# Feature DFT of an FNet branch as seven block products inside the attention, on one Trainium2 core

## The chip, the cores and the metric

The kernel runs on one core of a Trainium2 chip. The metric is device time in microseconds, from launch to end, as the median of several runs. TensorE (PE in the profile) multiplies, ScalarE (ACT), VectorE (DVE) and GpSimd (POOL) work elementwise, and SyncE (SP) issues nearly all DMA transfers from one queue, in order.

## The reference

Two branches read the same x (2048 tokens, 640 features) and are mixed by a gate per token.

```python
# A: attention with 32 heads of 20 features
qkv = x @ wqkv                       # 640 -> 3 x 640
scores = q @ k.T * 20 ** -0.5
a = softmax(scores) @ v              # per head, all 2048 x 2048 pairs
a = a.reshape(2048, 640) @ wo
# B: Fourier mixing, the DFTs given as matrices
re = x @ dft_hid_re.T                # 2048 x 640, the "feature DFT"
im = x @ dft_hid_im.T
b = dft_seq_re @ re - dft_seq_im @ im  # the "sequence DFT"
g = sigmoid((x * gate_w).sum(-1))
out = g * a + (1 - g) * b
```

All data are float32. A product of two such operands is made of three matmuls in the format fp32r: each operand is split into a high and a low part, and high x high, high x low and low x high are added in PSUM.

## The kernel before, in words

**The front (0 to 250 us).** x is loaded and split into eight blocks `x00` to `x13` (part z, token quarter t), laid out as 5 slices of 128 features by 512 tokens. Then come query and key rows for the first heads, the values (`v_pair`), and from 105.9 us the remaining 32 query/key tiles: `qk_tile` calls `qk_pairs`, where each of 15 pairs of matmuls has 64 features in the upper and 64 in the lower half of the array, with the sums in two PSUM banks. ScalarE copies one bank, VectorE adds the other, GpSimd makes high and low part (`split`), and SP stores both to `qk_scr` in HBM. Pair tiles (name `p`) have five buffers, the one-off `raw` tiles three, the split `part` tiles three, the wide weight tiles `wb` two.

Among these tiles stand the first ten (`HEAD`) of 64 feature-DFT tiles: `hid_first` runs `hid_tile`, 15 pairs of 320 columns for 128 tokens and a quarter of the outputs (half `hf` of the features, real or imaginary part `ri`). The result goes to `a_scr` in HBM. `tick` puts one score step of the row maxima (two matmuls at line 177, two maxima at line 179) into each tile, so that 43 (`LEAD`) steps are done when the attention begins.

**The attention (250 to 1841 us)** has 32 units (a pair of heads, half of the queries), in all 256 cycles of four score steps. The order of a cycle is written out by hand:

```python
ORDER = "emFemFFFFemFeFFmeFFemFFFmmFFmeeB"
```

"e" is a score matmul (line 912) whose exponential ScalarE takes (918); "m" is a score matmul for the row maxima of a later unit (177), reduced by VectorE (179); "F" is a share of the fills; "B" is the burst: the sixteen value matmuls of line 565 and up to two of the `extras`, the read-outs and additions that a fill has left. All "e" and "m" take turns in five PSUM banks, the fills have two of their own (`yp`).

The fills are, one after the other: the other 54 feature tiles (one cycle each), 7 products of the sequence DFT (168 cycles), which already works on halved operands with seven instead of eight block products (`PRODUCTS`), and 30 tiles of the output projection, one cycle each, the last `SLOW` = 4 of them two. From cycle 246 on no maxima are left and the order is `LATE`. `at_step` puts a DMA or an operation at a later score step, and `begin` and `end` call them. In the last feature cycles the first operands of the sequence DFT are loaded and split by GpSimd (`load_a_early`, `make_a_early`, `load_c`).

**The end (1841 to 1869 us)**: the last heads' normalization and the rest of the output projection.

Of the kernel before, what the change touches and what calls it, by code (L numbers as in the profile page):

```python
# [18 lines left out]
P = 128  # L19
# [24 lines left out]
MARKS = (7,)  # L44
HEAD = 10

# [13 lines left out]


LONG = (0, 0, 0, 0, 0, 0, 0)
FULL = 1
SLOW = 4
PRE = range(FULL, NS)
# [9 lines left out]
@with_exitstack  # L75
def mix_kernel(ctx: ExitStack, tc: tile.TileContext, xa, wqk, wb, cdft, wo, out):
    nc = tc.nc
# [19 lines left out]
    l_scr = dram.tile([NU, 4, 512], F32, name="l_scr")  # L97
    o_scr = dram.tile([D, S], F32, name="o_scr")
    m_scr = dram.tile([NU, P, 2, 32], F32, name="m_scr")

# [182 lines left out]

    def load_wqk(c):
        raw = raw_tile()[:, : ND * P].rearrange("p (d c) -> p d c", d=ND)
        sp.dma_start(raw, wqk[c])

        def finish():
            w = part_tile().rearrange("p z c -> p (z c)")[:, : 2 * ND * P].rearrange("p (z d c) -> p z d c", z=2, d=ND)
            split(w[:, 0], w[:, 1], raw, act, dve)  # L290
            wt[c] = w

        return finish
# [16 lines left out]

    stores, halves, hid_done = [], [], 0

# [4 lines left out]
    def qk_tile(c, t):  # L317
        if hid_done:
            return qk_pairs(c, t)
# [19 lines left out]

    def tick(pairs):  # L340
        if pairs in MARKS:
            run_s(min(step + 1, LEAD))

    def qk_pairs(c, t):
        w = wt[c]
        ps = two_banks()
        for d in range(ND):
            for z, (wz, xz) in enumerate(((0, 0), (0, 1), (1, 0))):
                for h in range(2):
                    r = slice(64 * h, 64 * h + 64)  # L350
                    pe.matmul(ps[h], w[r, wz, d], xs[xz][t][r, d], start=d == 0 and z == 0, stop=d == ND - 1 and z == 2)  # L351
                tick(3 * d + z + 1)
        if not halves:
# [31 lines left out]

    def hid_tile(i, read_out):
        j, st = divmod(i, NS)
        hf, ri = divmod(j, 2)
        yp[:] = two_banks() if i < HEAD else [new_y(0), new_y(1)]
        w = wt["b", 2 + j]  # L390
        t, cs = st // 4, slice(st % 4 * P, (st % 4 + 1) * P)
        for d in range(ND):
            for z, (xz, wz) in enumerate(((0, 0), (0, 1), (1, 0))):
                for h in range(2):
                    r = slice(64 * h, 64 * h + 64)
                    pe.matmul(yp[h][:, :HE], xs[xz][t][r, d, cs], w[r, wz, d, :HE],  # L396
                              start=d == 0 and z == 0, stop=d == ND - 1 and z == 2)
                if (d, z) != (ND - 1, 2):
                    yield
        a = raw_tile()[:, :HE]  # L400
        y0, y1 = yp[0][:, :HE], yp[1][:, :HE]

        def read():
            act.activation(a, y0, AF.Copy, scale=-1.0 if ri else 1.0)
            dve.tensor_tensor(a, a, y1, op=ALU.subtract if ri else ALU.add)  # L405

        read_out(read, (a_scr[ri, hf, st], a))
        yield


    def hid_first(i):
        def read_out(read, args):
            read()
            stores.append(args)

        for pairs, _ in enumerate(hid_tile(i, read_out)):
            tick(pairs + 1)

# [39 lines left out]
    for s in range(0, NS, 2):  # L458
        v_pair(1, s)
        if s == 0:  # L460
            fin = load_wb(2)
        if s == 6:
            fin()
            fin = load_wqk(order[1])
        if s == 12:
            fin()
            fin = load_wb(3)
    free[0] = range(2, 5)
    for n, c in enumerate(order):
        for t in range(4):  # L470
            m = 4 * n + t
            if m % 3 == 0 and hid_done < HEAD:
                hid_first(hid_done)
                hid_done += 1
            qk_tile(c, t)
            if m == 8:
                load_v(0)
            if t == 1:
                if n + 1 < len(order):
                    fin()  # L480
                if n + 2 < len(order):
                    fin = load_wqk(order[n + 2])
    free[0] = range(5)
    run_s(LEAD)
    flush()

    def make_gate():
# [13 lines left out]
    def a_tile(n, s):  # L501
        g, k = (n, s // 4), s % 4
        if g not in blocks or k in blocks[g][1]:
            b = 4 * n + s // 4
            blocks[g] = block(b % 2, b // 2).rearrange("p (k z c) -> p k z c", k=4, z=2), set()
        blocks[g][1].add(k)
# [6 lines left out]
    def load_c(g):  # L513
# [9 lines left out]
        def finish():  # L523
            c = cparts[g] = part_tile()
            if len(raws) > 1:
                pool.tensor_tensor(raws[0], raws[0], raws[1], op=ALU.add if PRODUCTS[n][0][1][0] > 0 else ALU.subtract)  # L526
            split(c[:, 0], c[:, 1], raws[0], pool, pool)

# [274 lines left out]
    goals, fins = {}, []  # L803
    def read_later(read, args):
        extras.append((now[0], read))
        at_step(now[0] + 2, functools.partial(sp.dma_start, *args))

    HID = 4 * NS - HEAD
    fills = itertools.chain(*(hid_tile(HEAD + g, read_later) for g in range(HID)), itertools.chain.from_iterable(dft_step(g) for g in range(NS * UNITS)),
                            itertools.chain.from_iterable(out_tile(tt, hf) for tt in PRE for hf in range(2)))  # L810

# [59 lines left out]
    def end(i):  # L871
        if i % 4 == 2:
            c = i // 4
            if c + HEAD in (NS, 2 * NS):
                at_step(i + 2, load_wb(3 + (c + HEAD) // NS, pool, pool))
            if c in (HID - 18, HID - 17, HID - 16):
                k = c - HID + 18
                load_a_early(6 * k, min(6 * k + 6, NS))
            if HID - 12 <= c < HID - 8 or HID - 8 <= c < HID - 4:
                at_step(i + 2, make_a_early)  # L880
                at_step(i + 4, make_a_early)
            if c in (HID - 7, HID - 5, HID - 3):
                at_step(i + 4, load_c((c - HID + 7) // 2))
        if i in LAST:
# [195 lines left out]
```

## Time and profile before

| | |
|---|---|
| median of 3 runs | 1871.31 us (1870.73 to 1871.7) |
| the profiled execution | 1871.24 us, span 1869.4 us, granted clock 0.999 |
| PE busy | 1859.3 us (99%), 18157 matmuls |
| DVE busy | 1468.8 us (79%) |
| ACT busy | 1223.4 us (65%) |
| POOL busy | 1077.1 us (58%) |
| DMA | 281.66 MB, mean 151 GB/s |

A row of groups gives line, engine, operation, output <- input, shapes and count, then busy time in us and mean ns of one, then the idle time of the engine before them and who ended it. A row of windows gives the stretch, its length, and for PE, PEld (weight loads), DVE, ACT and POOL the busy time and the count, then the granted clock, the DMA engines' mean busy share and GB/s; where it is taken for one line, only the engines of that line appear. A row of the timeline gives start and length in us of a merged run of instructions.

### The profile page before, as it was taken

What the parts mean: (1) busy time and instruction counts of PE and PEld (TensorE: products, weight loads), DVE (VectorE), ACT (ScalarE), POOL (GpSimd) and SP (SyncE); (2) the same over time, 40 slices, a digit from 0 to 9 for tenths busy, and PEclk for the clock granted to TensorE, in tenths of its full rate; (3) what the DMA queues carried; (4) which work ended last, traced back from release to release, by engine and by line L of the source; (5) the groups of instructions that cost most, each with busy time, mean ns of one, the idle gap of its engine ahead of it and who ended that gap; (6) DMA issues with size and microseconds to landing.
All of it is one profiled execution on the core that took longest, in us unless ns stands there. A gap on an engine that the chain in (4) does not pass through costs nothing. (4 is left out here: it accounts for less than half of the span.)

```text
span 1869.4 us, 46025 instructions
## 1 busy us (share of the span) xinstructions
PE 1859.3 (99%) x18157; PEld 1356.1 (73%) x18157; DVE 1468.8 (79%) x2436; ACT 1223.4 (65%) x2359; POOL 1077.1 (58%) x942
## 2 busy tenths in 40 slices
PE   9999999999999999999999999999999999999998
PEld 8988877777777677776777767777677776766665
DVE  4145679898988888888888888888888888889943
ACT  4221257777777677676776767767677676777785
POOL 1234421010046896566799899777789988634434
PEclk9999999999999999999999999999999999999999
DMA  7744341312325473536666576647476746342214
GB/s 234 181 136 149 140 135 45 88 53 75 108 73 194 146 239 113 164 124 190 207 185 220 174 255 184 175 132 198 147 237 197 209 163 203 114 101 78 63 44 152
DMA packets 182283, 281.66 MB, mean 151 GB/s; under 512 B 52799, under 2 KB 114367, under 8 KB 182067
## 3 DMA queue, kind: packets, MB, share of 16 engines
q1 hardware_dynamic: 181107, 276.75, 49.2%
q0 software_dynamic: 960, 1.97, 0.6%
q8 instruction: 143, 2.34, 0.5%
q14 instruction: 73, 0.60, 0.1%
HBM read 213.90 MB, written 64.57 MB: 149 GB/s over the span
## 5 line engine op out<-in xcount | busy, mean ns | idle before, releaser
L179 DVE TENSOR_REDUCE mx<-ps 128x1 f32<-128x512 f32 x2048 | 1297.9, 684 | 200.0 <-PE ps L177 179.7
L918 ACT ACTIVATE p<-ps 128x512 f32<-128x512 f32 x2048 | 1087.0, 599 | 423.8 <-PE ps L177 217.0
L177 PE MATMUL ps<-kst,qst 60*128 60x512 f32 x2048 | 782.7, 413 | 0.9 <-DVE mx L179 0.6
L912 PE MATMUL ps<-qst,kst 62*128 62x512 f32 x2048 | 699.1, 415 | 0.2
L646 PE MATMUL yp<-x,part 64*128 64x320 f32 x5376 | 642.7, 306 | 0.0
L646 PEld LDWEIGHTS yp<-x,part 64*128 64x128 f32 x5376 | 580.5, 186 | 7.5
L912 PEld LDWEIGHTS ps<-qst,kst 62*128 62x128 f32 x2048 | 333.4, 184 | 225.5 <-DVE mx L179 169.8
L565 PE MATMUL av<-p,v 128*21 128x512 f32 x4096 | 492.5, 596 | 0.0
L177 PEld LDWEIGHTS ps<-kst,qst 60*128 60x128 f32 x2048 | 372.7, 184 | 11.0 <-DVE mx L179 1.4
L117 POOL TENSOR_TENSOR part<-raw,part 128x1024 fp32r<-128x1024 f32 (+1 forms) x129 | 290.6, 2253 | 10.3
L565 PEld LDWEIGHTS av<-p,v 128*21 128x21 f32 x4096 | 95.6, 100 | 206.9 <-issue 205.9
L396 PE MATMUL yp<-wb,x 64*128 64x320 f32 x1920 | 228.5, 307 | 0.0
L526 POOL TENSOR_TENSOR raw<-raw,raw 128x1024 f32<-128x1024 f32 x77 | 185.9, 2414 | 43.7 <-DMA raw<-in_cdft 42.1
L116 POOL CAST part<-raw 128x1024 fp32r<-128x1024 f32 (+1 forms) x129 | 127.1, 986 | 140.3 <-PE yp L646 119.3
L396 PEld LDWEIGHTS yp<-wb,x 64*128 64x128 f32 x1920 | 204.7, 186 | 3.7 <-DVE raw L405 0.2
L595 POOL TENSOR_TENSOR o<-o,rb 128x512 f32<-128x512 f32 x31 | 40.2, 1295 | 150.4 <-ACT p L918 52.7
L717 PE MATMUL yp<-x,part 64*128 64x320 f32 x720 | 90.3, 309 | 0.0
L117 POOL TENSOR_TENSOR x<-araw,x 128x320 fp32r<-128x320 f32 x96 | 83.9, 874 | 7.7
L351 PE MATMUL ps<-x,part 64*128 64x512 f32 x630 | 84.0, 390 | 0.0
L717 PEld LDWEIGHTS yp<-x,part 64*128 64x128 f32 x720 | 77.7, 186 | 2.9
L351 PEld LDWEIGHTS ps<-x,part 64*128 64x128 f32 x630 | 65.4, 185 | 11.3
L734 POOL TENSOR_TENSOR x<-x,m 128x320 f32<-128x320 f32 x30 | 26.2, 873 | 80.1 <-DVE m L729 63.9
(92 smaller groups left out, 1150.5 us busy)
## 6 DMA issues: line engine op xcount, KB each, us to landing
raw<-in_cdft SPq DMA_DIRECT2D x192, 512.0 KB
araw<-a_scr SPq DMA_DIRECT2D x176, 160.0 KB
qk_scr<-p SPq DMA_DIRECT2D x40, 512.0 KB
kst<-qk_scr SPq DMA_DIRECT2D x90, 160.0 KB
qst<-qk_scr SPq DMA_DIRECT2D x90, 160.0 KB
a_scr<-raw SPq DMA_DIRECT2D x64, 160.0 KB
yt<-y_scr SPq DMA_DIRECT2D x64, 160.0 KB
y_scr<-yt SPq DMA_DIRECT2D x64, 160.0 KB
```

Of the source, the lines that this page charges most:

```text
L116: e1.tensor_copy(dst1, src)
L117: e2.tensor_tensor(dst2, src, f32(dst1), op=ALU.subtract)
L177: pe.matmul(ps, q[b : b + KROWS, qt * P : (qt + 1) * P], k[b : b + KROWS, kc * 512 : (kc + 1) * 512], start=True, stop=True)
L179: return lambda: dve.tensor_reduce(mx[n][:, h, qt, kc : kc + 1], ps, axis=AX.X, op=ALU.max)
L351: pe.matmul(ps[h], w[r, wz, d], xs[xz][t][r, d], start=d == 0 and z == 0, stop=d == ND - 1 and z == 2)
L396: pe.matmul(yp[h][:, :HE], xs[xz][t][r, d, cs], w[r, wz, d, :HE], start=d == 0 and z == 0, stop=d == ND - 1 and z == 2)
L526: pool.tensor_tensor(raws[0], raws[0], raws[1], op=ALU.add if PRODUCTS[n][0][1][0] > 0 else ALU.subtract)
L565: pe.matmul(av[32 * j : 32 * j + DH + 1, :], v[:, kt, h * (DH + 1) : (h + 1) * (DH + 1)], pp[qc][:, h, :], start=kt == 0, stop=kt == NS - 1)
L646: pe.matmul(yp[h][:, :HE], c[r, cz, cs], a[r, az], start=s == 0 and z == 0, stop=s == NS - 1 and z == 2)
L717: pe.matmul(yp[h][:, :HE], o[r, oz, d], wos[d, hf][r, wz], start=d == 0 and z == 0, stop=d == ND - 2 and z == 2)
L912: pe.matmul(pt, k[b : b + KROWS + 2, kt * P : (kt + 1) * P], q[b : b + KROWS + 2, qc * 512 : (qc + 1) * 512], start=True, stop=True)
L918: act.activation(pts[n, kt, qc][:, h], pt, AF.Exp, scale=float(DH) ** -0.5)
```

## The change

The feature DFT is written as one product of a 2 x 2 block matrix x (token half by feature half) with a 2 x 2 block matrix of weights (feature half by real or imaginary part), and that as seven products of sums of blocks, each added to up to two results. A product has 8 units (half `hf` of the outputs, `k` of four token tiles), 56 in all. With only 320 features to sum over, a unit works on two token tiles at once, one in each half of the array, in 15 pairs of the same matmul shape as before. None is ahead of the attention; the fills begin with them, one cycle each.

- Weights (right operands): `load_set` loads one or two blocks of each of 14 sets, GpSimd adds them, ScalarE and GpSimd split them, and they go to `w_scr`; this runs beside the query/key tiles. `load_right` brings a set back, once into each half of the partitions, four cycles ahead.
- Left operands: `load_left` loads one or two blocks of x (a new input `xh`), GpSimd adds and splits slab by slab, into the blocks of x that are free by then, one product ahead; the first one at the end of the front.
- Results: two of the four stay in SBUF (`acc`), the other two are kept in `a_scr`, loaded again for the second addition. The read-out multiplies by the product's sign: ScalarE reads one bank, VectorE the other; GpSimd adds. Bursts of the feature stage may run three extras.
- The front: `SLOW` is 2; 14 query/key tiles have two score steps (`TWICE`), so that 43 are done as before; the high part of a query/key tile is made by ScalarE instead of GpSimd, the low part of the query/key weights by GpSimd instead of VectorE; the last eight tiles are taken in another order, the token quarters 2 and 3 first.
- The first operands of the sequence DFT are loaded and split later, in the last nine feature cycles, and lie in other blocks.

The core of the diff:

```diff
-HEAD = 10
+TWICE = range(2, 16)
+FEATURE = (
+    (((1, 1, 1),), ((1, 1, 0), (-1, 0, 0)), 1.0, ((1, 0, 0), (1, 1, 0))),
+    (((1, 0, 0), (1, 1, 1)), ((1, 0, 0), (-1, 1, 1)), 1.0, ((1, 0, 0), (1, 1, 1))),
+    (((1, 1, 0), (1, 1, 1)), ((1, 0, 0),), 1.0, ((1, 1, 0), (-1, 1, 1))),
+    (((1, 0, 0),), ((1, 1, 1), (-1, 0, 1)), 1.0, ((1, 0, 1), (1, 1, 1))),
+    (((1, 0, 0), (1, 0, 1)), ((1, 1, 1),), -1.0, ((-1, 0, 0), (1, 0, 1))),
+    (((1, 0, 1), (-1, 1, 1)), ((1, 1, 0), (-1, 1, 1)), 1.0, ((1, 0, 0),)),
+    (((1, 1, 0), (-1, 0, 0)), ((1, 0, 0), (-1, 0, 1)), 1.0, ((1, 1, 1),)),
+)
+SETS = 2 * len(FEATURE)
+RW = ND * HE
-SLOW = 4
+SLOW = 2
...
-        split(st[:, 0].bitcast(R), st[:, 1].bitcast(R), raw, pool, pool)
+        split(st[:, 0].bitcast(R), st[:, 1].bitcast(R), raw, act, pool)
...
+    def load_set(k):
+        _, terms, _, _ = FEATURE[k // 2]
+        w = wide.tile([P, 2, ND, BW], R, name="wb", bufs=2).rearrange("p z d c -> p (z d c)")
+        half = RW // 2
+        raws = [f32(w)[:, half * i : half * i + half] for i in range(2)]
+        for raw, (_, dh, ri) in zip(raws, terms):
+            sp.dma_start(raw, wr[ri, dh, k % 2])
+        def add():
+            if len(terms) > 1:
+                pool.tensor_tensor(raws[0], raws[0], raws[1], op=ALU.add if terms[1][0] > 0 else ALU.subtract)
+        def finish():
+            split(w[:, 2 * half : 3 * half], w[:, 3 * half : 4 * half], raws[0], act, pool)
+            stores.append((w_scr[k].rearrange("z r (q c) -> (r q) z c", q=2),
+                           f32(w)[:, 2 * half : 4 * half].rearrange("p (z c) -> p z c", z=2)))
+    def load_right(k):
...
+        for h in range(2):
+            sp.dma_start(f32(w)[64 * h : 64 * h + 64], w_scr[k].rearrange("z r c -> r z c"))
...
+    def hid_pair(u):
+        n, hf, k = u // 8, u // 4 % 2, u % 4
+        _, _, factor, targets = FEATURE[n]
+        ps = [new_y(z)[:, :HE] for z in range(2)]
...
+        for d in range(ND):
+            for a, b in ((0, 0), (0, 1), (1, 0)):
+                for z in range(2):
+                    r = slice(64 * z, 64 * z + 64)
+                    pe.matmul(ps[z], lefts[n][a][r, d, k * P : k * P + P], rights[2 * n + hf][r, b, d],
+                              start=done_ == 0, stop=done_ == 3 * ND - 1)
...
+        def read():
+            act.activation(m[:, 0], ps[0], AF.Copy, scale=factor)
+            dve.tensor_scalar(m[:, 1], ps[1], factor, 1.0, op0=ALU.mult, op1=ALU.mult)
+        def add(sign, old):
+            pool.tensor_tensor(old, old, m, op=ALU.add if sign > 0 else ALU.subtract)
+        extras.append((now[0], read))
+        last = n == len(FEATURE) - 1
+        for (sign, th, ri), new, row, old in zip(targets, fresh, rows, olds):
+            if not new:
+                extras.append((now[0] + 3, functools.partial(add, sign, old)))
+            if th != ri or ri == 0 and n == len(FEATURE) - 2 or ri == 1 and last:
+                at_step(now[0] + (4 if new else 8), functools.partial(sp.dma_start, row, m if new else old))
...
+    tiles = [(n, t) for n in range(6) for t in range(4)] + [(n, t) for t in (2, 3, 0, 1) for n in (6, 7)]
+    for m, (n, t) in enumerate(tiles):
+        qk_pairs(order[n], t, m)
+        if m == 8:
+            load_v(0)
+        if sets:
+            sets[0][m % 2]()
+            if m % 2:
+                sets.pop(0)
+            elif 2 <= m < 2 * SETS - 2:
+                flush()
+                sets.append(load_set(m // 2 + 1))
+        if n < 6 and t == 1:
+            fin()
+            if n + 3 < len(order):
+                fin = load_wqk(order[n + 3], pool)
+        if m == 27:
+            slabs = load_left(0, raw_stage)
+        if m in (28, 30):
+            flush()
+            load_right((m - 28) // 2)
+        if m >= 27:
+            slabs.pop(0)()
...
-    HID = 4 * NS - HEAD
+    HID = 8 * len(FEATURE)
...
+                if c % 4 == 0 and 2 <= c // 4 + 1 < SETS:
+                    at_step(i + 1, functools.partial(load_right, c // 4 + 1))
+                if k == 0 and n + 1 < len(FEATURE):
+                    slabs.extend(load_left(n + 1, own_stage))
+                if slabs:
+                    slabs.pop(0)()
...
-        run_extras(max(done - HIDS, 0) // 3, 2)
+        run_extras(max(done - HIDS, 0) // 3, 3 if c <= HID else 2)
```

More of the change, by code (lines that the diff above doesn't have):

```diff
@@ L526, in finish, with load_c_first @@
                 pool.tensor_tensor(raws[0], raws[0], raws[1], op=ALU.add if PRODUCTS[n][0][1][0] > 0 else ALU.subtract)
+            split(c[:, 0], c[:, 1], raws[0], pool, pool)
+        return finish
+    c_raws = []
+    def load_c_first(g):
+        if not c_raws:
+            w = f32(wide.tile([P, 2, ND, BW], R, name="wb", bufs=2)).rearrange("p z d c -> p (z d c)")
+            c_raws.extend(w[:, 1024 * q : 1024 * q + 1024] for q in (0, 1, 2, 0))
+        (_, th, ri), (sign, th2, ri2) = PRODUCTS[0][0]
+        raws = [c_raws.pop(0) for _ in range(2)]
+        for raw, (half, part) in zip(raws, ((th, ri), (th2, ri2))):
+            o = (2 * part + g % 2) * 1024
+            sp.dma_start(raw, cdft[half * HT + g // 2, :, o : o + 1024])
+        def finish():
+            c = cparts[g] = part_tile()
+            pool.tensor_tensor(raws[0], raws[0], raws[1], op=ALU.add if sign > 0 else ALU.subtract)
             split(c[:, 0], c[:, 1], raws[0], pool, pool)
```

171 lines of the change are left out of this document (100 added, 71 removed).

## The prediction

> **What bounds the kernel now.** I read the page first (slices, groups), then windows over the bursts of the value product (line 565: sixteen matmuls end each cycle of the attention), then one cycle in the timeline, then the front.
>
> ```profile
> span 1869.4 us, 46025 instructions
> PE   9999999999999999999999999999999999999998
> DVE  4145679898988888888888888888888888889943
> POOL 1234421010046896566799899777789988634434
> ```
>
> TensorE is busy everywhere, which doesn't say that it sets the pace everywhere. The windows of line 565, each beginning just ahead of a burst:
>
> ```profile
> 257.30:507.80 250.50, 76.89 (x640) 14.78 (x640) 1.00 0.28 79
> 526.52:589.20 62.68, 19.20 (x160) 3.73 (x160) 1.00 0.40 123
> 589.20:1650.30 1061.10, 322.91 (x2688) 62.13 (x2688) 1.00 0.60 179
> 1650.30:1785.00 134.70, 42.31 (x352) 8.11 (x352) 1.00 0.32 84
> 1796.00:1805.78 9.78, 3.89 (x32) 0.76 (x32) 1.00 0.25 67
> 1810.38:1836.96 26.58, 11.49 (x96) 2.79 (x96) 1.00 0.38 100
> ```
>
> Divide each stretch by its bursts (x640 is 40): feature cycles with 15 pairs of fill matmuls take 6.26 us, those at the end of that stage, beside a busy GpSimd, 6.27; sequence-DFT cycles with 16 pairs 6.32; output cycles with 12 pairs 6.12. Four pairs more or less move a cycle by 0.2 us, so the pairs are mostly filling. In the last cycles no maxima are left: 4.89 us with 12 pairs, 4.43 with 6. One feature cycle in the timeline:
>
> ```profile
> 269.79 1.92 PE L565 MATMUL av<-p,v 128*21 128x512 f32 x16
> 269.83 1.28 DVE L179 TENSOR_REDUCE mx<-ps 128x1 f32<-128x512 f32 x2
> 270.81 0.45 ACT L404 ACTIVATE raw<-yp 128x320 f32<-128x320 f32 x1
> 271.29 0.49 DVE L405 TENSOR_TENSOR raw<-raw,yp 128x320 f32<-128x320 f32 x1 [0.19 <-ACT raw L404]
> ...
> 271.64 0.51 PE L177 MATMUL ps<-kst,qst 60*128 60x512 f32 x1
> ...
> 272.20 5.13 DVE L179 TENSOR_REDUCE mx<-ps 128x1 f32<-128x512 f32 x8 [0.42 <-PE ps L177]
> ```
>
> Eight maxima run without a gap for 5.13 us (0.64 each); then VectorE has 1.09 us, from 271.11 to 272.20, in which it can get no new maximum because TensorE is in the burst. The read of the feature tile (0.49) lies in that hole. 5.13 + 1.09 is the cycle: VectorE's maxima and the burst set it.
>
> The front is different. From 105.9 to 250.0 us come 32 query/key tiles and ten feature tiles:
>
> ```profile
> 133.84 1.29 PE L396 MATMUL yp<-wb,x 64*128 64x320 f32 x13
> ...
> 147.34 1.29 PE L396 MATMUL yp<-wb,x 64*128 64x320 f32 x13
> ```
> ```profile
> 238.76 1.77 PE L351 MATMUL ps<-x,part 64*128 64x512 f32 x14
> 240.36 0.40 PE L177 MATMUL ps<-kst,qst 60*128 60x512 f32 x2
> 240.60 2.01 PE L351 MATMUL ps<-x,part 64*128 64x512 f32 x16
> 242.44 1.77 PE L351 MATMUL yp<-x,part 64*128 64x512 f32 x14
> ```
>
> Here TensorE runs without holes: a query/key tile with its one score step takes 242.44 - 238.76 = 3.68 us, the step in it 0.24, and one feature tile with three query/key tiles 147.34 - 133.84 = 13.50. What TensorE no longer does here is time saved.
>
> **The sum, part by part.** *Ten feature tiles leave the front.* One costs 13.50 - 3 x 3.68 = 2.46 us, less its score step, which only moves to another tile (43 steps before and after): 2.22. Ten: -22.2. The weight halves 2 and 3 are no longer split there, and with them goes one stall:
>
> ```profile
> 117.53 3.32 DVE L117 TENSOR_TENSOR wb<-raw,wb 128x966 fp32r<-128x966 f32 x2 [0.21 <-ACT wb L114]
> ...
> 121.50 0.18 PEld L177 LDWEIGHTS ps<-kst,qst 60*128 60x128 f32 x1 [0.94 <-DVE mx L179]
> ```
>
> VectorE split weights until 120.85, its maxima came late and TensorE waited 0.9: -0.9. The tile stretch shrinks from 144 to 121 us.
>
> *The feature stage.* Seven products of 8 units, 15 pairs each, are 840 pairs instead of 960; but the cycles count, not the pairs. It takes 56 cycles instead of 54, the end gives back two (only the last two output tiles, not four, get two cycles). Two output cycles become feature cycles: 2 x (6.26 - 6.12) = +0.3. Four late cycles get 12 pairs instead of 6: 4 x (4.89 - 4.43) = +1.8.
>
> *A unit's read-out.* Now ScalarE and VectorE each read one bank, neither waiting for the other; VectorE's operation changes from 0.49 to the kind of the second row:
>
> ```profile
> L405 DVE TENSOR_TENSOR raw<-raw,yp 128x320 f32<-128x320 f32 x64 | 31.1, 486 | 11.8 <-ACT raw L404 11.8
> L728 DVE TENSOR_SCALAR m<-yp,gate 128x320 f32<-128x320 f32 x7 | 3.9, 551 | 39.3 <-PE yp L717 36.2 <-PE ps L912 3.1
> L358 DVE TENSOR_TENSOR p<-p,ps 128x512 f32<-128x512 f32 x21 | 14.4, 687 | 23.7 <-ACT p L357 23.7
> L117 POOL TENSOR_TENSOR p<-p 128x512 fp32r<-128x512 f32 x32 | 42.2, 1320 | 2.6
> L117 POOL TENSOR_TENSOR part<-raw,part 128x512 fp32r<-128x512 f32 x15 | 19.4, 1290 | 1.2
> L116 POOL CAST part<-raw 128x512 fp32r<-128x512 f32 x15 | 9.2, 613 | 10.9 <-PE yp L646 5.7 <-PE ps L912 3.7 <-PE ps L177 1.4
> L117 POOL TENSOR_TENSOR part<-raw,part 128x640 fp32r<-128x640 f32 x1 | 1.6, 1568 | 0.1
> L117 POOL TENSOR_TENSOR wb<-raw,wb 128x966 fp32r<-128x966 f32 x2 | 4.5, 2275 | 0.2
> ```
>
> 0.55 in a hole of 1.09 costs nothing; without that cover it would be 56 x 0.06 = 3.4. Nor does the wait that goes (0.19) give anything, since the next maximum waits for TensorE. A rule speaks against this operation beside a GpSimd that is now busy. The Trainium skill ("SBUF — State Buffer", Who interferes with whom) says that a tensor-scalar operation of VectorE in its two-port mode and GpSimd shut each other out of the shared port; "VectorE: DVE Perf Modes" (Mode 2×_2P) restricts that mode to operands in SBUF, and this one reads a PSUM bank. The row fits the restriction: 551 ns for 320 columns is no faster than the two-input kind.
>
> *GpSimd in the feature stage.* A unit's add to an old result, 128x640, takes 1.57 us; a half-operand slab of 128x512 takes 1.29 for the sum of two blocks and 0.61 + 1.29 for the split. The fullest product with slabs (the fifth) has 16 adds, 5 slabs and one normalization: 25.1 + 16.0 + 1.3 = 42.4 us in its 8 x 6.26 = 50.1. Operands are ready two cycles ahead of their use, sums have a cycle before they are stored. So it is hidden; the two feature windows above (6.26 and 6.27) show that a busier GpSimd doesn't move the cycle. I take +1, with 0 and 5.6 (0.1 per cycle) as ends; fewer pairs show 0.14 less per cycle, so -3 as the end below. What queues behind a waiting SP instruction: the store of a sum waits for GpSimd, and the loads of the next heads and of the row of maxima stand behind it; but it is issued two cycles after the unit, a cycle after its add.
>
> *What the front gains in load.* Fourteen weight sets are loaded, added, split, stored to HBM. GpSimd: 32 low parts at 1.32, 24 operations of 128x800 at about 1.9 (an estimate between the 640 and 966 rows), six weight splits at 1.57, five slabs at 1.9: 42 + 46 + 9 + 10 = 107 of 121 us. VectorE in a tile with two steps: 4 x 0.64 + 0.69, plus some 0.6 in which its add waits for ScalarE's copy: 3.9 us beside TensorE's 3.68 + 0.24 = 3.92. Both fit barely. The DMA is tighter: 32 stores of 512 KB (16.8 MB), 20 block loads of 0.41 (8.2), 14 set stores of 0.82 (11.5), six weight tiles (2.0), values, first left operand and two duplicated right operands (4.9): 43.4 MB in 121 us, 359 GB/s.
>
> ```profile
> 105.90:249.60 143.70, 143.11 (x1353) 122.72 (x1354) 87.19 (x136) 28.71 (x51) 63.08 (x62) 1.00 0.39 141
> 23.00:33.00 10.00, 9.55 (x58) 8.83 (x58) 5.27 (x6) 5.28 (x9) 0.00 (x0) 1.00 0.96 359
> 904.00:924.00 20.00, 20.00 (x205) 14.32 (x202) 16.80 (x27) 14.14 (x27) 17.86 (x14) 1.00 0.86 295
> ```
> ```profile
> qk_scr<-p SPq DMA_DIRECT2D x31, 512.0 KB
> ```
>
> The front now moves 141 GB/s. The best ten microseconds of the trace reach 359, with 512 KB loads and stores like those here; a 20 us stretch of smaller packets 295. At 359 nothing is lost; at 295 the front takes 147 us, +26. On SP, which issues everything in order, each set load waits until the set two before it has landed in HBM, and the query/key stores queue behind that; they have five buffers of pair tiles, over two tiles (7 us) of grace. I take +2, near the 359 row because the transfers are of its kind; ends 0 and +26. "DMA: Bandwidth & Descriptors" in the Trainium skill (Specifications) gives 358 GB/s from HBM per core; by that figure the transfers would need 121 us, the same as TensorE, and the +2 would stand.
>
> *The joint.* The last slab of the first left operand comes after the last tile, some 5 us of GpSimd work (its low part, two slabs) before the twelfth pair of the first unit needs it: about even, +1 (0 to 3).
>
> Sum: -22.2 - 0.9 + 0.3 + 1.8 + 1 + 2 + 1 = -17.0. The profiled execution took 1871.24 us (1.8 outside its span), 0.07 below the median of 1871.31. Forecast 1854, in a range of its own from 1846 (no front loss, no joint, -3 in the feature stage) to 1859.
>
> **Rivals.** *The front becomes DMA-bound* (the one that ends slower): it decides below 43.4 MB / (121 + 19) us = 310 GB/s. At 295 the +2 becomes +26: 1878. For it: nothing in the trace holds 359 for more than about ten microseconds, and a load that waits for a store to land leaves a hole on the only queue. Against it: the buffers' grace and the sets with a single block. Half way, 310 to 345 GB/s, 1860 to 1867; around 310 nothing changes.
>
> *GpSimd sets the cycle in the feature stage*: if two adds and a slab (3.14 + 3.2 = 6.3) run in series with the unit's read (0.45), 6.8 instead of 6.26 in the 15 such cycles of three products, +8: 1862. For it, the sums; against it, three cycles without slabs in each product.
>
> *VectorE sets the front*: 0.35 us more in each of the 14 tiles with two steps: +5, 1859.
>
> *The port is locked after all*: each read waits for a GpSimd add or is waited for, 0.55 + 1.57 - 1.09 = 1.0 per cycle, 56 of them: 1910. The row at 551 ns speaks against it. The Trainium skill's rule of the shared port is its ground.
>
> **How the numbers follow.** A measurement of this kernel can tell about 0.2% (3.7 us) from no change. Forecast 0.64, front half bound 0.08, GpSimd 0.05, VectorE 0.04: faster 0.81. Front bound at about 310 GB/s: same 0.05. Front bound below that 0.10, port 0.04: slower 0.14. The range 1846 to 1868 takes in all the faster cases and leaves out 0.19.
>
> **What would show it.** Right: attention begins near 227 us, TensorE without waits in the front, windows of line 565's successor at 6.26 to 6.3 us a cycle in the feature stage. Wrong: TensorE or ScalarE in the front waiting behind pair tiles, a DMA share near 0.9 there with tiles over 3.9 us; feature cycles over 6.4 us; a wait of the score matmuls for left operands or for the row of maxima.

## The result, and the profile after

| | before | after |
|---|---|---|
| median | 1871.35 us (1870.73 to 1871.7) | 1895.83 us (1891.53 to 1901.53) |
| profiled execution, span | 1871.24, 1869.4 us | 1897.29, 1895.5 us |
| granted clock | 0.999 | 0.990 |
| DMA | 281.66 MB | 348.81 MB |

The ratio is 1.0133 (95% interval 1.0105 to 1.0161): slower by 24 us where 17 less were forecast. Four points of the trace divide the spans: the first score matmul (front before it, joint behind it), the first burst of the value product (line 701 in the new kernel), burst 56, and the last one. In us against the kernel before; the last column is a kernel that stands at the end of the experiments:

| stage | forecast | after | last kernel |
|---|---|---|---|
| front, to the first score matmul (before: 250.0) | -21.1 | -10.9 | -21.8 |
| joint, to the first burst (before: 7.3) | +1 | +9.1 | +5.8 |
| 56 feature cycles against the first 56 before (350.9) | +1.3 | +27.6 | +1.0 |
| cycles 56 to 246 | 0 | +1.5 | +1.7 |
| the rest | +1.8 | -1.2 | -0.9 |
| sum | -17.0 | +26.1 | -14.2 |

The front and the joint gave 18 us less than forecast, and the feature cycles lost 26. The windows of line 701 (columns: PE, PEld, granted clock, DMA share, GB/s) show that these cycles aren't slower as such:

```profile
297.00:391.10 94.10, 28.77 (x240) 5.61 (x240) 1.00 0.62 158
397.40:417.00 19.60, 5.23 (x32) 0.91 (x32) 0.83 0.75 220
497.30:531.90 34.60, 9.52 (x64) 1.58 (x64) 0.85 0.76 214
633.90:1696.00 1062.10, 322.90 (x2688) 61.98 (x2688) 1.00 0.62 181
```

Fifteen bursts in 94.10 us are 6.27 each, as forecast; the sequence DFT has its 6.32. But the next rows take 19.6 us for two cycles (22 and 23, counted from zero by the burst that begins them) and 34.6 for four. The first of them, engine by engine (PE, PEld, DVE, ACT, POOL):

```profile
397.40:403.40 6.00, 6.00 (x62) 4.18 (x60) 5.23 (x10) 4.57 (x9) 0.69 (x1) 1.00 0.80 194
403.40:409.40 6.00, 0.90 (x8) 0.43 (x7) 2.00 (x4) 0.04 (x1) 4.91 (x4) 0.67 0.49 137
409.40:413.20 3.80, 3.80 (x23) 1.04 (x24) 0.01 (x1) 1.80 (x4) 2.06 (x3) 0.62 0.82 263
```

TensorE does nearly nothing for 5 us, and then the clock is 0.62: 23 matmuls fill 3.80 us. (The Trainium skill, "TensorE: Matmul & The Clock Gate", Part 1, has the clock halved after an idle window of some 3.4 us; the rows agree, and so a wait costs more than its own length: the two cycles take 7.1 us more than plain ones, TensorE stood for 5.1 of it.) The waits (engine, line, releaser; total, times, longest) name what was late, and SP's queue says why:

```profile
PE ps L1052 <- DMA qst<-m_scr: 13.1, 3, 6.7
SPq L489 <- DMA a_scr<-part: 31.5, 8, 8.2
```
```profile
388.57 0.41 SPq L991 DMA_DIRECT2D a_scr<-part  x1
389.07 2.82 SPq L423 DMA_DIRECT2D wb<-w_scr  x2
393.22 0.37 SPq L489 DMA_DIRECT2D part<-a_scr  x1
393.68 0.93 SPq L991 DMA_DIRECT2D a_scr<-part  x1
394.70 0.42 SPq L724 DMA_DIRECT2D r_scr<-lc  x1
395.17 0.42 SPq L234 DMA_DIRECT2D m_scr<-m  x1
403.40 0.37 SPq L489 DMA_DIRECT2D part<-a_scr  x1
403.82 0.46 SPq L991 DMA_DIRECT2D a_scr<-part  x1
404.37 2.85 SPq L240 DMA_DIRECT2D qst<-m_scr  x4
```

Read it backwards. A unit's score matmuls need its row of maxima, which goes to HBM (`m_scr`) and comes back into `qst`. The matmul waits for this row (line 240), issued at 404.37 although its data were stored at 395.17. Ahead of it in SP's order stands the load of an old sum (489), which waits until 403.40 because the sum that lay in its place, stored at 393.68, has not landed. That store stands in the DMA behind the right operand, two transfers of 800 KB issued at 389.07. The DMA is full meanwhile, at a low rate:

```profile
392.00:399.00 7.00, 7.00 (x82) 4.61 (x74) 6.46 (x13) 5.17 (x11) 3.08 (x2) 1.00 1.01 222
```

The row is late three times. Cycles 22, 23, 38 and 39 carry 16.6 of the 27.6 us that the feature cycles take more than the kernel before's, the waits and the slow clock behind them. Cycle 35 carries 4.9: there VectorE stands 3.7 us for the row of the exponentials' sums (`lc`, line 721), which also comes through SP. Cycle 4 carries 3.5 for which the profile names no releaser.

In the front SP stands in the same way, at the set loads (line 404):

```profile
SPq L404 <- DMA w_scr<-wb: 47.4, 12, 6.1
ACT wb L128 <- POOL wb L408: 25.0, 6, 7.8
```
```profile
200.57 0.41 SPq L329 DMA_DIRECT2D w_scr<-wb  x1
201.07 0.84 SPq L329 DMA_DIRECT2D qk_scr<-p  x1
205.02 0.85 SPq L404 DMA_DIRECT2D wb<-in_wr  x2
205.97 0.38 SPq L329 DMA_DIRECT2D qk_scr<-p  x1
206.44 0.41 SPq L329 DMA_DIRECT2D w_scr<-wb  x1
206.95 1.00 SPq L329 DMA_DIRECT2D qk_scr<-p  x1
213.44 0.82 SPq L404 DMA_DIRECT2D wb<-in_wr  x2
```

A set goes out at 206.44; the next load into its tile is issued only at 213.44. GpSimd's add is then late, ScalarE stands for it (25.0 us in all) with the next query/key tile's copy behind, and TensorE runs out of PSUM banks, while the DMA isn't full (columns: all five engines, clock, DMA share, GB/s):

```profile
195.00:220.00 25.00, 18.36 (x139) 13.95 (x137) 7.94 (x13) 6.83 (x11) 14.44 (x10) 0.93 0.77 267
```

### The profile page after: what moved, and what is told of

The parts are those of the page before. It is cut to its first block, busy times and chain, and to the rows that moved or that the text cites. A ratio compares the mean times of both kernels' runs of the same rounds, so it can differ in the third digit from the quotient of the medians.

```text
span 1895.5 us, 45927 instructions
## 1 busy us (share of the span) xinstructions
PE 1853.7 (98%) x17917; PEld 1340.8 (71%) x17917; DVE 1453.8 (77%) x2420; ACT 1248.2 (66%) x2392; POOL 1293.3 (68%) x1092
## 2 busy tenths in 40 slices
DMA packets 205820, 348.81 MB, mean 184 GB/s; under 512 B 54319, under 2 KB 124079, under 8 KB 205603
## 5 line engine op out<-in xcount | busy, mean ns | idle before, releaser
L131 POOL TENSOR_TENSOR part<-raw,part 128x1024 fp32r<-128x1024 f32 (+3 forms) x134 | 296.9, 2216 | 15.0 <-ACT part L128 4.8
L496 PE MATMUL yp<-wb,x 64*128 64x320 f32 x1680 | 212.6, 312 | 7.7 <-POOL p L131 4.5
L130 POOL CAST part<-raw 128x1024 fp32r<-128x1024 f32 (+2 forms) x127 | 125.0, 984 | 134.1 <-PE yp L782 102.6
L496 PEld LDWEIGHTS yp<-wb,x 64*128 64x128 f32 x1680 | 183.7, 190 | 11.7 <-POOL p L131 4.8
L509 POOL TENSOR_TENSOR x<-x,raw 128x640 f32<-128x640 f32 x40 | 62.4, 1561 | 39.5 <-DVE raw L506 30.8
L363 PE MATMUL yp<-x,part 64*128 64x512 f32 x480 | 66.0, 398 | 7.2 <-ACT p L369 6.0
L676 POOL TENSOR_TENSOR araw<-araw 128x320 f32<-128x320 f32 x80 | 69.9, 874 | 1.9 <-DMA araw<-a_scr 1.9
```

The costliest lines, as they stand in the source:

```text
L130: e1.tensor_copy(dst1, src)
L131: e2.tensor_tensor(dst2, src, f32(dst1), op=ALU.subtract)
L496: pe.matmul(ps[z], lefts[n][a][r, d, k * P : k * P + P], rights[2 * n + hf][r, b, d], start=done_ == 0, stop=done_ == 3 * ND - 1)
```

## The experiments

The theory: SP's one queue is blocked in two ways, by a load that waits until a store out of the same place has landed, and by a slow block that stands in the DMA ahead of small transfers. The rivals: the bytes alone fill the DMA (V), or GpSimd is the late engine (G). Each time below is the median of 4 to 10 executions; but for a single outlier, those of one kernel lie up to 14 us apart, so that a difference of a few us between two medians says little. In the code, `...` stands for lines that are not shown.

**Fixed set tiles.** The two tiles are taken once and used by region, so that a block load waits only for the split that read its region.

```diff
...
-        w = wide.tile([P, 2, ND, BW], R, name="wb", bufs=2).rearrange("p z d c -> p (z d c)")
+        if k < 2:
+            set_tiles.append(wide.tile([P, 2, ND, BW], R, name="wb", bufs=2).rearrange("p z d c -> p (z d c)"))
+        w = set_tiles[k % 2]
```

> The right operand's sets use two tiles by region for the whole front: a set's blocks load into the first half of a tile as soon as the split of two sets before has read it, and no longer wait for that set's store to land. Theory T: the front's 12 us of stalls come from SP standing at the block load until the store has landed (34.8 us on SP in seven places), GpSimd's add being late and ScalarE's first part standing in front of the next tile's copy: 1882 to 1887, the first score matmul at 227 to 230 us instead of 239. Rival V (the front's bytes fill the DMA): 1891 to 1901, with the stalls on other waits. Rival G: GpSimd's add and split (4 us and more per set) are the limit, no change.

1886.02 us, ratio 1.0081 (1.0066 to 1.0096), 9.8 us less. The first score matmul comes at 228.4 instead of 239.1, and the same window has TensorE busy and the DMA at its full share:

```profile
195.00:220.00 25.00, 24.02 (x207) 21.24 (x205) 11.65 (x18) 9.59 (x16) 19.70 (x14) 1.00 1.03 382
```

The whole kernel moves the same 348.81 MB as the changed one: the order of the queue, not the bytes, held the front. All kernels below but the next have this edit. In the profiled executions of the nine kernels that have this edit and practically the same front, the first score matmul comes at 228.3 to 233.1 us, so that up to 5 us in a single trace's front say nothing about an edit.

**The row of maxima on GpSimd's queue** (on the changed kernel).

```diff
+        rq = sp if now[0] < 0 else pool
...
-            sp.dma_start(m_scr[n], f32(m))
+            rq.dma_start(m_scr[n], f32(m))
... # and rq for the row's four loads
```

> Within the attention the row of maxima (its store and its four loads) is issued by GpSimd's queue instead of SP's; nothing else changes. Theory T (SP's order, not the DMA, holds the row): the score matmuls' wait for the row (13.1 us in three places) and the slow bursts behind it go, some 20 us; what is left is the wait for the reciprocal's row (3.7 us) and the front; 1872 to 1880. Rival V (DMA too full): the row lands as late from another queue, 1891 to 1901. Rival G (GpSimd is the late engine): its queue gives the row even later, over 1897.

1945.96 us, ratio 1.0397 (1.0380 to 1.0415). The waits:

```profile
POOL qst L242 <- DMA m_scr<-m: 64.3, 22, 7.1
PE ps L1054 <- DMA qst<-m_scr: 43.0, 11, 10.0
```

GpSimd now stands for the landing of the row's own store, and the row is later still. The time lies where rival G put it (over 1897), but by a wait that the edit itself brought: the run doesn't decide between them.

**Later loads of old sums**: three steps after the pair's begin, stores two steps earlier.

```diff
-                sp.dma_start(old, row)
+                at_step(now[0] + 3, functools.partial(sp.dma_start, old, row))
...
-                at_step(now[0] + (4 if new else 8), ...
+                at_step(now[0] + (4 if new else 6), ...
```

> On top of the fixed set tiles (1886.0 us), the load of an old sum is issued three steps after its pair's begin and not at it, and a sum is stored two steps earlier, so that five steps (7.8 us) and not none lie between a store and the next load of the same place; bytes and engines are as they were. Theory T, part Q (SP stands at the load until the store before it has landed, 24.8 us in six waits, and the rows of maxima and of sums of the exponentials stand behind): the waits for the row of maxima (13.2 us) and the slow bursts behind them go, 1866 to 1872. Part D alone (the rings are held): the rows are late all the same, 1882 to 1889. Rival V: 1882 to 1889.

1894.56 us: 8.5 *more*. Of the 12.3 us between the two profiled executions 6.4 are in the feature cycles; 4.4 are in the front, which the edit doesn't touch. The waits for the row stay (14.2 us in three places). In cycle 22 SP stood instead at a sum's store, which waits for GpSimd's add, which waits for the old sum: its load was issued at 379.48, behind the right operand, and the add began at 389.86. Without the wait at line 489 the row is as late; the block in front is enough to hold it.

**Right operands in two transfers over all partitions**, the rows of one part read for both halves.

```diff
-        for h in range(2):
-            sp.dma_start(f32(w)[64 * h : 64 * h + 64], w_scr[k].rearrange("z r c -> r z c"))
+        for z in range(2):
+            sp.dma_start(f32(w)[:, z], w_scr[k, z : z + 1].to_broadcast([2, 64, RW]))
```

> On top of the fixed set tiles (1886.0 us), each right operand is fetched by two transfers over 128 partitions (the high parts, then the low parts; the source rows read twice), in place of two over 64 partitions of the same bytes. Theory T, part D (the transfers over half the partitions run at half rate and hold the rings for about 7.5 us): the stalls of the feature stage (cycles 22, 35, 38 and 54, some 21 us over the plain 6.25) shrink by half, 1873 to 1879. If only SP's order matters (part Q), no change: 1883 to 1889. Rival V (volume): no change.

2190.67 us, ratio 1.1706 (1.1685 to 1.1727): a failed experiment, for a reason of its own, so that it says nothing about the theory. A window within such a transfer:

```profile
381.00:400.00 19.00, 11.76 (x115) 7.81 (x112) 11.11 (x19) 9.22 (x18) 9.70 (x9) 0.93 0.13 53
```

A share of 0.13 is two engines of sixteen. (The Trainium skill, "DMA: Bandwidth & Descriptors", Why a DMA increments its semaphore by 16 and not by 1, says that a transfer uses the largest number of engines up to 16 that divides the slowest dimension of both sides; here the source's is 2, and the share agrees.) The two kernels that held the same transfer, with later loads and with an earlier joint, took 2195.56 and 2197.91 us and tell nothing more.

> Both edits on top of the fixed set tiles: later loads of old sums and right operands over 128 partitions. Theory T: 1864 to 1870, a little under the better of the two, since both shorten the same wait. Rival V: 1880 or more.

> As the kernel with both edits, and the first left operand's slabs and the first two right operands start one token tile earlier in the front, so that they are there when the first feature pair starts. Theory T: the 7 to 9 us that lie between the first score matmul and the first value matmul beyond the kernel before's 7.3 shrink by 3 to 6 us: 1859 to 1866. Rival: the front's DMA is full there (share over 1.0 from 195 us on) and the tiles before it lose what the joint gains: within 1.5 us of the kernel without it.

**The same bytes over 128 different rows**, which puts half of them where another part belongs, so that the kernel doesn't give the wanted output and only prices the transfer; and three ways to move the block in time or place:

```diff
# 128 rows, in wrong places
+        for j in range(2):
+            sp.dma_start(f32(w)[:, j], w_scr[k].rearrange("z r c -> (z r) c"))
# four pieces: half h, part z
+        for j, (h, z) in enumerate(itertools.product(range(2), range(2))):
+            args = f32(w)[64 * h : 64 * h + 64, z], w_scr[k, z]
...
+                at_step(now[0] + 3 * j, functools.partial(sp.dma_start, *args))
# GpSimd's queue (rq is GpSimd within the attention)
+            rq.dma_start(f32(w)[64 * h : 64 * h + 64], w_scr[k].rearrange("z r c -> r z c"))
# two cycles later
-                if c % 4 == 0 and 2 <= c // 4 + 1 < SETS:
+                if c % 4 == 2 and 2 <= c // 4 + 1 < SETS:
```

> On top of the fixed set tiles, each right operand is fetched by two transfers of 800 KB over 128 different rows and 128 partitions; the rows are put in the wrong places, so that the operand is not the one wanted; bytes, packets and queue are as before. Theory B with the half rate as its cause: the block takes 4.5 to 5 us and not 8 to 9, the waits for the row of maxima (13.2 us) halve or go, 1868 to 1878. If 64 or 128 partitions make no difference: 1882 to 1889.

> On top of the fixed set tiles (1886.0 us), each right operand is fetched in four pieces of 400 KB (half of the partitions, one part each), three steps (4.7 us) apart, in place of 1.6 MB at once; same bytes, still over 64 partitions. Theory B (a block of 1.6 MB at some 210 GB/s stands in the queue's rings for 8 to 9 us; the sums' stores and loads behind it land late, SP stands for them in order, and the row of maxima behind SP comes late): a piece holds the rings for 2 us, the four long cycles (22, 35, 38, 54; some 21 us) shrink to a few us, 1866 to 1873. Rival V (the DMA's volume, whatever its order): 1882 to 1889. Rival Q (SP's order and waits alone, however the blocks lie): 1880 to 1889.

> On top of the fixed set tiles, the right operands' loads within the attention are issued by GpSimd's queue instead of SP's, so that they stand in rings of their own. Theory B (the order within the queue's rings is what delays the small transfers): sums and rows go past the block, 1866 to 1874. If the sixteen engines are full for the block's time whichever queue it comes from: 1882 to 1889. Rival G: GpSimd stands for the tile to come free and its adds are late: 1885 or more.

> On top of the fixed set tiles, each right operand's load is issued two cycles later (two cycles before its first use and not four), behind the row of maxima of the units in question and not ahead of it. Theory B: cycles 22 and 38, which wait for the row (some 16 us with the slow bursts behind them), become plain ones; 1868 to 1877. Rival V: 1882 to 1889; a late operand (score pairs waiting for it) would show as TensorE waiting for the operand's load, over 1889.

The 128 rows: 1863.49 us, ratio 0.9962 (0.9946 to 0.9978), 22.5 us less than the fixed sets and faster than the kernel before, with the same bytes. In the profiled executions 18.6 us of the gain are in the feature cycles. The waits of the fixed sets (first two rows) and of this kernel:

```profile
PE ps L1056 <- DMA qst<-m_scr: 13.2, 3, 6.9
SPq L493 <- DMA a_scr<-part: 32.2, 8, 8.1
```
```profile
PE ps L1056 <- DMA qst<-m_scr: 1.6, 1, 1.6
SPq L493 <- DMA a_scr<-part: 26.1, 8, 4.1
```

The longest wait of SP for a sum's landing is halved, and the row is hardly late any more. The others (pieces, GpSimd's queue, later load) took 1892.41, 1896.99 and 1909.27 us, none less than the fixed sets' 1886.02. What TensorE waits for in them:

```profile
PE yp L504 <- DMA wb<-w_scr: 27.9, 7, 10.1
PEld yp L504 <- DMA wb<-w_scr: 23.8, 4, 10.5
```
```profile
PE yp L500 <- DMA wb<-w_scr: 40.8, 14, 5.8
```

The first two rows are the pieces, the third the later load. In both, cycles 22 and 38 are plain (6.26 to 6.27 us): the block did hold the row. But at its rate the operand then comes too late itself. On GpSimd's queue TensorE still waits for the row (16.2 us in three places) and GpSimd stands 29.3 us for the operand's tile to come free. So what helped was the rate, and none of these places. Volume (V) is out here, since the bytes are the same, and so is GpSimd (G), whose work is the same too.

**Why the rate.** Two other ways to fill both halves: the halves on two queues at once, or three parts in the scratch (high, low, high), of which rows 0 to 127 and 64 to 191 are fetched; the other half of the array then finds the parts exchanged.

```diff
# two queues
-            sp.dma_start(f32(w)[64 * h : 64 * h + 64], w_scr[k].rearrange("z r c -> r z c"))
+            q = sp if h == 0 or now[0] < 0 else act
+            q.dma_start(f32(w)[64 * h : 64 * h + 64], w_scr[k].rearrange("z r c -> r z c"))
# three parts
-    w_scr = dram.tile([SETS, 2, 64, RW], F32, name="w_scr")
+    w_scr = dram.tile([SETS, 3, 64, RW], F32, name="w_scr")
... # the high part is stored a second time
+        for j in range(2):
+            sp.dma_start(f32(w)[:, j], w_scr[k, j : j + 2].rearrange("z r c -> (z r) c"))
...
-                    pe.matmul(ps[z], lefts[n][a][r, d, k * P : k * P + P], rights[2 * n + hf][r, b, d],
+                    pe.matmul(ps[z], lefts[n][a][r, d, k * P : k * P + P], rights[2 * n + hf][r, b ^ z, d],
```

> On top of the fixed set tiles (1886.0 us), the upper half of each right operand within the attention is issued by ScalarE's queue and the lower half by SP's, so that the two transfers over 64 partitions each run at the same time, from rings of their own. Theory P (one transfer over half of the partitions is bounded by what that half takes in, some 210 GB/s, and two at once over different halves are not): the block takes 4.5 to 5 us and not 8 to 9, the time comes near the 1863.5 us of the misplaced rows: 1864 to 1874. If the bound is on the source's side (each row read by one engine at its own pace): 1880 to 1889. ScalarE's issue costs at most 0.65 us each on a queue of exponentials, 12 times.

> On top of the fixed set tiles, the scratch of the right operands holds high, low and high parts (the high part stored twice, 5.7 MB more in the front), and each operand is two transfers over 128 different rows: high over low, low over high; the lower half's matmuls take the parts in the other order. Every result is the wanted one. Theory P: the feature stage is that of the misplaced rows (348 us for 55 cycles), and the front pays for 5.7 MB more, at the 316 GB/s of its first stretch at most 18 us and, beside its share of 0.81 to 0.89, some 3 to 8: 1866 to 1872. If the misplaced rows were fast for another reason than the partitions: 1885 or more.

Two queues: 1890.65 us, no gain and outside the 1864 to 1874 that the theory gave. Half a block alone on the DMA, then both halves together:

```profile
300.00:302.00 2.00, 2.00 (x20) 0.63 (x14) 1.33 (x3) 1.24 (x3) 0.54 (x1) 1.00 1.04 208
413.00:417.00 4.00, 4.00 (x50) 3.37 (x50) 3.96 (x7) 3.28 (x7) 3.94 (x4) 1.00 1.07 295
```

ScalarE's half and SP's were issued 1 to 16 us apart, so they seldom ran together, and the time doesn't decide; where they met, 295 GB/s, some small transfers included. Three parts: 1871.94 us, ratio 1.0002 (0.9993 to 1.0012), 14.1 less than the fixed sets although 5.7 MB more are stored in the front. Its block:

```profile
377.00:381.00 4.00, 4.00 (x48) 3.82 (x44) 3.57 (x7) 3.15 (x6) 3.56 (x3) 1.00 1.04 413
```

208 to 222 GB/s into 64 partitions (222 with a few other transfers in the window), 413 into 128, with all engines busy in both. The source isn't the difference: with the 128 misplaced rows each transfer reads the same 128 rows of HBM as before, and the kernel's packets are as many (205820, against 205821). The partitions that a transfer goes to set its rate. The Trainium skill ("SBUF — State Buffer", Door 1) says that partitions 0 to 63 reach 8 of 16 ports, 196 GB/s for 1 MiB and 218 at most; the rows agree. The Trainium skill ("SBUF — State Buffer", "Can I just issue two DMAs to hit both halves?") says that two transfers into different halves gain 6%; 295 against 208 is more, in one window that other transfers share.

**The joint and the rest of the front.** The first left operand and the first two right operands one token tile earlier:

```diff
-        if m == 27:
+        if m == 26:
...
-        if m in (28, 30):
+        if m in (27, 29):
...
-            load_right((m - 28) // 2)
+            load_right((m - 27) // 2)
```

> The misplaced rows (1863.5 us, output not the wanted one), and the first left operand's slabs and the first two right operands one tile earlier in the front. Theory T: what the joint has beyond the kernel before's shrinks by 3 to 6 us: 1857 to 1861. Rival: the front's DMA is full there, the tiles before lose what the joint gains: 1862 to 1866.

> Three parts and the earlier joint together, a kernel that computes what is wanted. Theory: 1861 to 1869, 3 to 6 us under the one without the earlier joint. Rival (the front's DMA, with 5.7 MB more, is the bound): no gain, or a loss, from starting earlier: 1868 to 1876.

1868.71 and 1877.31 us: no gain, but 5 us more each, the first within the spread of its executions. The joint didn't shrink (18.4 us with the misplaced rows, 15.2 without the edit). Then, on the kernel with the misplaced rows, fewer bytes or less work ahead of it:

```diff
# second blocks not loaded
-        for raw, (_, dh, ri) in zip(raws, terms):
+        for raw, (_, dh, ri) in zip(raws, terms[:1]):
... # the first block is added to itself, GpSimd works as long
# no adds, both blocks loaded
-            if len(terms) > 1:
-                pool.tensor_tensor(raws[0], raws[0], raws[1], op=ALU.add if terms[1][0] > 0 else ALU.subtract)
```

> The misplaced rows (1863.5 us; first value matmul 244.5 us), and the second block of the ten two-term sets is not loaded (4 MB fewer in the front; the first block is added to itself, so GpSimd does as much as before; output not the wanted one). Theory F (from 195 us on the front's DMA is full, share 1.02 to 1.03): the front and the joint end 5 to 9 us sooner, near the 235 us of the forecast: 1854 to 1859. Rival G (GpSimd's add and split, 104 of 133 us, are what ScalarE and the joint wait for): 1861 to 1866.

> The misplaced rows, and GpSimd does not add the two blocks of a set (ten adds of 128 x 800, some 1.9 us each; both blocks are loaded, the first alone is split; output not the wanted one). Theory F: the front is bound by bytes at its end, 1860 to 1866. Rival G: the waits for GpSimd's add (9.3 us on ScalarE) go, 1854 to 1859.

1863.13 and 1865.91 us, against 1863.49: neither. The first score matmul comes at 227.5 and 226.1 instead of 229.3. The prediction named 227, so the tile stretch has little more to give; the joint is 13.9 and 16.0. What keeps it at twice the kernel before's is in part open. In the last kernel's trace TensorE stands there mainly for the first right operand, issued only at 223.67, and its weight loads for GpSimd's slab of the left operand (window 226 to 243):

```profile
PE yp L502 <- DMA wb<-w_scr: 4.1, 2, 2.1
PEld yp L502 <- POOL x L130: 2.3, 1, 2.3
```

The clock falls behind these waits, and the DMA is full throughout, with the next left operand, right operands and key rows:

```profile
226.00:230.00 4.00, 3.16 (x23) 2.28 (x19) 1.31 (x3) 1.56 (x3) 3.92 (x4) 1.00 1.03 393
230.00:234.00 4.00, 0.60 (x1) 0.28 (x1) 0.19 (x1) 0.78 (x2) 3.84 (x6) 0.62 1.00 344
```

That these bytes make the operand late wasn't tried.

**A version that beats both.** Three parts, but the second high part of sets 2 to 13 is copied in HBM during the attention; then the later loads of old sums, two steps and with the stores where they were.

```diff
+                if c % 4 == 0 and c // 4 + 2 < SETS:
+                    at_step(i + 7, functools.partial(sp.dma_start, w_scr[c // 4 + 2, 2], w_scr[c // 4 + 2, 0]))
# and, in the second kernel
...
-                sp.dma_start(old, row)
+                at_step(now[0] + 2, functools.partial(sp.dma_start, old, row))
```

> As the kernel with three parts (1871.9 us), but the second high part of sets 2 to 13 is not stored in the front; it is copied within the scratch memory during the attention, one set ahead (12 copies of 400 KB, by SP's queue). Every result is the wanted one. Theory: the front is again that of the fixed sets with whole operands (first value matmul 244 to 246 us), the feature stage stays near 350 us; the copies' 0.8 MB each are hidden beside it: 1863 to 1869. Rival: the copies delay the rows behind them as the half transfers did: 1872 to 1885.

> As the kernel with the copies, and the load of an old sum two steps after its pair's begin. Theory Q (SP still stands some 7 us for a sum's store in cycle 38, where the misplaced rows and the three parts have one long cycle of 8.2 to 11.8 us): that cycle shrinks too, 2 to 6 us under the kernel with the copies alone: 1859 to 1866. Rival (the later load makes the add and the next store late, as it did with the half transfers, +8.6): above it.

1866.19 us, ratio 0.9971 (0.9959 to 0.9984), and 1857.97 us, ratio 0.9929 (0.9915 to 0.9944), 13.5 us less than the kernel before, with the wanted output. It moves 354.54 MB, more than the changed kernel. The 56 feature cycles take 6.28 us each on average; only the first (6.89) is over 6.6, and TensorE no longer waits for the row of maxima:

```profile
241.31:593.23 351.92, 107.66 (x896) 20.72 (x896) 1.00 0.67 220
```

The wait at line 489 was a cause too, but a second one: the kernel with the later load is 8.5 us slower behind the slow block and 8.2 faster without it. Which of the two differences between the edits (the stores' step, the block's rate) turns the sign wasn't tried apart.

## Why the prediction was wrong

- **Ten tiles leave the front, -22.2, and the stall, -0.9**: right in kind and size. With fixed sets the first score matmul comes 17 to 22 us earlier (228.3 to 233.1), in most traces 20 or more.
- **The front's load, +2**: the step that failed first. It measured +12 (10.9 gained, not 23.1). The prediction saw that a set load waits for a store's landing on SP and took the five pair tiles as its grace. The grace covers the query/key stores; the late load is passed on another way, through GpSimd's add to ScalarE, which takes the set's high part ahead of the next tile's copy. The rival "DMA-bound below 310 GB/s" has the right sign, but not the mechanism: the fixed sets ran at 382 GB/s where the changed kernel had 267. That is also more than the 359 of the row that the prediction took for the best, and than the 358 that it quotes beside it; the block's 4 us had 413.
- **The joint, +1 (0 to 3)**: +9.1, and +5.8 in the best kernel. The sum counted GpSimd's slabs and not the wait for the first right operand (2.9 us in the changed kernel, 4.1 in the best). Why that comes late is open.
- **The cycle, 6.26 to 6.3 us, and two cycles exchanged, +0.3**: right: 6.27 where nothing waits, and 351.9 for 56 in the best kernel against 350.9.
- **The read-out, 0**: right. VectorE's operation took 0.48 us, not 0.55, and no row shows a locked port: all 56 lie between 0.480 and 0.483 us beside a busy GpSimd. In the best kernel the eight cycles without adds, but for the first, and the 48 behind them take 6.23 to 6.53.
- **GpSimd in the feature stage, +1, and SP beside it, 0**: the step that failed worst, 26 us. It asked whether a sum's *store* would hold up the row of maxima and priced that at nothing. It didn't ask about the sum's *load*, which waits for the store before it, nor what stands in the DMA ahead of that store. And it has no term for the right operands of this stage, 1.6 MB each: 7.4 us at the 222 GB/s of half of the partitions, where 128 need 4.0 at 413.
- **Late cycles, +1.8**: +1.0 for the cycles. The 4.89 us came from a window of two cycles, one of 5.04 and one of 4.74; the added ones take 4.74. The end behind them is 1.9 to 2.2 us shorter, which no term had; why is open.
- **Prices of the rivals**: two don't come out of their own numbers. At 345 and 310 GB/s the 43.4 MB give 1857 and 1871, not 1860 and 1867; and two adds per unit occur in two products (the third and the fifth), not three, which makes GpSimd's rival 10 cycles and +5. Neither moves the forecast.
- **What would show it wrong**: "a wait of the score matmuls for left operands or for the row of maxima" came, for the row, but no rival had it as its mechanism, and its price, with the clock's fall behind it, was missing. In the front the share was 0.83 to 0.94, as that sign says, but 0.77 in the 25 us in which TensorE stood most.

## What to carry over

In a queue that issues in order, price each transfer that waits for another to land by what stands *in the DMA* ahead of that one, and list the small urgent rows behind it. A transfer into 64 partitions counted nearly double here (222 GB/s against 413). Where moving a block only moves the stall, look at its rate first; an edit that failed before that can gain after it.

## What the runs showed of the hardware

A transfer into half of the partitions kept all engines busy (share 1.0) at 208 to 222 GB/s, one into all of them reached 413. A source whose outer dimension is 2 ran on 0.13 of the engines, 53 GB/s. Around and after 5.1 us with hardly any matmul the granted clock was 0.62 to 0.67, and the two cycles took 7.1 us more than plain ones, 2 more than the wait itself.
